# Last weight's low halves made by TensorE in the bank of its norms, in a one-core kernel of top-k attention and two ReLU² networks

## The chip, the cores and the metric

The program runs on one core of one Trainium2 chip. The metric is device time of one execution in microseconds. The kernel before takes 1182.04 us (median of three runs, 1180.84 to 1185.24).

## The reference, cut to what matters

```
q, k, v: (4, 8, 576, 64) f32       # batch, heads, sequence, head_dim
scores = q @ k.T / 8               # per batch and head
keep the 32 largest of each row of 576, softmax over them, attn = p @ v
x  = attn laid out as 2304 tokens x 512
x1 = (s * relu(x  @ moe_w_in )**2 + b) @ moe_w_out     # 512 -> 2048 -> 512
x2 =      relu(x1 @ moe2_w_in)**2      @ moe2_w_out    # 512 -> 2048 -> 512
```

The four weights arrive as 64-bit words (float64 bits). The kernel makes float32 of them on the chip.

## The kernel before, in words

The 2304 tokens are cut into 18 tiles of 128. Tile 4 and tile 13 (counted from 0) hold 64 rows each of two batches. For each tile the eight attention heads are done one by one, 144 in all; the text below counts heads from 1. A head is: Q times K on TensorE (`f_qk`, L594, into one of two `pS` banks), four rounds of the eight largest on VectorE (`max` L605, `match_replace` L616), exp on ScalarE (L619), the mask and the row sum on VectorE (L643), a float16 pair of high and low halves (ScalarE L646, GpSimd L451), a transposing DMA, and P times V on TensorE (`f_av`, L659).

A tile that has its eight heads goes to network 1 (`ffn(u, 0, ...)`) and later to network 2 (`ffn(u, 1, ...)`). The units of tiles are named F00 to F014 for network 1 (eleven single tiles, three pairs, one single) and F10 to F19 for network 2 (one single, eight pairs, one single). A unit has 16 chunks of the inner 2048: twelve matmuls in (`f_in`, L762), ReLU and two squares on ScalarE (L771, L773, L776), the low half on GpSimd (L781), and three matmuls out for each tile (`f_out`, L799).

Every matrix product is made with float16 pairs (high half, low half). So each of the four weights, numbered 0 to 3, is prepared once, in 16 chunks of 128 x 512: a load; two or three VectorE operations that put the float64 bits together (L884, L893, L900), with ScalarE and GpSimd helping where the table `CONV` says T (L889, then L451 by `po27`); a `gram` matmul (`f_mm`, L947) that sums squares into the bank `pC[1]`; after each group of chunks (one group for weights 0 and 1, two for 2, four for 3) a scale from the largest column norm (`weight_scale`: L955, L957, L959); and then `split_w`, which writes the halves. `SPLIT` says how, chunk by chunk:

- O: ScalarE scales the chunk (L912) and casts it (L913), GpSimd subtracts (L451).
- U: ScalarE makes the high half (L915), GpSimd scales the chunk (L929) and subtracts (L451).
- P: ScalarE makes the high half (L915); TensorE forms the difference in a PSUM bank from a scaled diagonal `dgs` and minus one times the high half (`f_sub`, L922 and L923); ScalarE copies it out (L926).

Weights 0 and 1 are split by P, weight 2 by O and U in turn, weight 3 by O. Weight 3 is not kept on the chip: its halves are stored to device memory (`wo2`) and read back in pairs of chunks through the two `wring` buffers for every unit of network 2. `column_sums` (L1059) adds up weight 1's halves on TensorE, also in `pC[1]`, for the constant b of network 1.

Nothing runs in the order in which it is written. `Plan.add` records each operation with an engine, a cost, a priority, what it reads and what it writes; the order of writing alone sets the dependencies (a bank or buffer that two operations share). `Plan.order` then builds one fixed queue for each engine with a list scheduler that goes by costs and priorities. The priority is a number of heads, plus what the table `TW` adds for the operation's name and its tag. Each engine works through its queue in order and waits where its next operation isn't ready.

Of the kernel before, what the change touches and what calls it, by code (L numbers as in the profile page):

```python
# [34 lines left out]
SPLIT = ('P', 'P', 'OU', 'O')  # L35
# [7 lines left out]
HW = 1  # L43
# [4 lines left out]
X2F = 14  # L48
WB = 3
CSP = 12  # L50
# [3 lines left out]
LN = 9  # L54
WO2S = 0
# [8 lines left out]
QP = 8  # L64
# [214 lines left out]
def kernel(  # L279
# [191 lines left out]
    def pair_sums(b, j, prio, raws):  # L471
        for a, (raw, rn) in enumerate(raws):
            add(act, "ac1", 0.86, prio, lambda raw=raw, a=a: nc.scalar.activation(
                out=junk, in_=raw.rearrange("p c d -> p (c d)"), func=ACTF.Square,
                accum_out=kst[:, b, j, a:a + 1]), r=[rn, rn + "m"], w=[f"kst{b}{j}{a}"])
# [20 lines left out]
    def prep_pair(b, j, prio):  # L496
# [7 lines left out]
        for a, (raw, rn) in enumerate(raws):  # L504
# [8 lines left out]
            add(act, "ac3", 0.64, prio, lambda raw=raw, dst=dst: nc.scalar.copy(dst[:, :, 0, :], raw),  # L513
# [11 lines left out]
    def prep_q(t, prio):  # L525
# [15 lines left out]
        add(act, "ac4", c_act(DM), prio, lambda: nc.scalar.activation(  # L541
# [8 lines left out]
        add(act, "ac6", c_act(DM), prio, lambda: nc.scalar.copy(nat[:, :, 0, :], raw3), r=names, w=[nh])  # L550
# [116 lines left out]
    def split_x(n, prio, xt_i, tt, sc, si):  # L667
# [3 lines left out]
        add(act, "ac14", c_act(DM), prio, lambda: nc.scalar.activation(  # L671
# [5 lines left out]
        add(act, "ac16", c_act(DM), prio, lambda: nc.scalar.copy(nat[:, 0:DM], x), r=[f"xs{n}"], w=[f"xnh{n}"])  # L677
# [229 lines left out]
    def split_w(o, on, hi, lo, hn, ln, wi, c, prio):  # L907
# [20 lines left out]
        if way == "U":  # L928
            add(pool, "po29", 0.81, prio, lambda: nc.gpsimd.tensor_scalar(o, o, sc, None, op0=ALU.mult), r=[scn] + hn, w=on)  # L929
        on_pool("po30", prio, lo, o, hi, DM, HW, on + hn, ln)  # L930

    def gram_place(wi):

        if wi > 1 and "P" in SPLIT[wi]:
            return pH[:, 258:386], pH[:, 384:512], "pG"
        return pC[1][:, 0:128], pC[1][:, 384:512], "pC1"
# [220 lines left out]
```

## Time and profile before

| what | value |
|---|---|
| median of three runs | 1182.04 us |
| the profiled execution, its own time | 1180.55 us |
| its span in the profile | 1178.8 us |
| TensorE matmul busy | 1023.8 us (87%) |
| VectorE busy | 968.4 us (82%) |
| ScalarE busy | 878.8 us (75%) |
| GpSimd busy | 705.1 us (60%) |
| chain that ended last, by engine | PE 48%, DVE 10%, DMA 8%, ACT 6% |

The profile gives busy time of each engine over the whole span or over stretches of it, the groups of instructions with count and mean, what ended the idle time before each, and the chain of work that ended last. Shares over the whole span hide that the program has stages: weights and the first tiles (to about 320 us), attention with both networks beside it (to 1017 us), and a rest of network work alone.

### The profile page before, as it was taken

Reading aid. Unit: us, or ns where it says so; the run is one execution under the profiler, and the core shown is the slowest. Engines: PE = TensorE matmul, PEld = TensorE weight load, DVE = VectorE, ACT = ScalarE, POOL = GpSimd, SP = SyncE. Lnnn points to the kernel's source line nnn. Section 1 sums busy time; section 2 is a strip of 40 time slices with the busy share of each in tenths; the row PEclk is TensorE's granted clock in tenths of the full one; section 3 lists DMA queues with packets and bytes.
Section 4 is the critical chain, followed back from the end, with each engine's and each line's share of the span. In section 5 each row is a group of like instructions: output and inputs, shape, how many; then the busy total and the mean of one; then the engine's idle time right before and its main releaser. Section 6 shows DMA issues by size and latency. Waiting matters only on the chain.

```text
span 1178.8 us, 27766 instructions
## 1 busy us (share of the span) xinstructions
PE 1023.8 (87%) x10000; PEld 691.4 (59%) x10000; DVE 968.4 (82%) x2126; ACT 878.8 (75%) x2242; POOL 705.1 (60%) x1121
## 2 busy tenths in 40 slices
PE   1376757678989999998999999999999999999996
PEld 1233335446657667666666676666666676666664
DVE  6999999999998999999999999997999999510000
ACT  3478757779889878878997899868877687565644
POOL 4577299888667645755776567646654464442322
PEclk9979978889999999999999999999999999999999
DMA  8778954566966773585488636676386256233134
GB/s 256 236 227 204 232 168 116 161 179 157 221 126 134 164 174 65 122 203 139 92 151 199 133 75 131 160 175 123 79 165 159 50 144 166 46 69 121 28 115 145
DMA packets 338218, 171.16 MB, mean 145 GB/s; under 512 B 292512, under 2 KB 317088, under 8 KB 338080
## 3 DMA queue, kind: packets, MB, share of 16 engines
q1 hardware_dynamic: 338080, 169.39, 60.1%
q8 instruction: 78, 1.28, 0.5%
q14 instruction: 60, 0.49, 0.1%
HBM read 89.65 MB, written 8.91 MB: 84 GB/s over the span
## 4 chain that ended last, share of the span: by engine, by line
PE 48%; DVE 10%; DMA 8%; ACT 6%; issue 2%; POOL 2%; SPq 1%; POOLq 0%; ACTq 0%; DVEq 0%
PE pC L799 20%; PE pH L762 18%; DVE m L605 5%; PE pA L659 4%; DMA pT<-pn 4%; PE pC L762 3%; PE pS L594 3%; DMA wring<-wo 2%; DVE wk L616 2%; DVE spare L616 2%; DVE et L643 1%; ACT rr L771 1%; DMA xT<-xn 1%; DMA out_dram<-xs 1%; DMA qT<-knat 1%
## 5 line engine op out<-in xcount | busy, mean ns | idle before, releaser
L762 PEld LDWEIGHTS <-w 128*128 128x128 f16 x4800 | 366.2, 99 | 103.1 <-issue 40.9
L762 PE MATMUL pH<-xT,w 128*128 128x256 f16 (+1 forms) x3648 | 371.2, 252 | 23.5 <-ACT rr L771 19.3
L451 POOL TENSOR_TENSOR pn<-et,pn 128x576 f16<-128x576 f32 x144 | 185.8, 1292 | 49.0 <-ACT pn L646 35.3
L781 POOL TENSOR_TENSOR gl<-gg,gh 128x128 f16<-128x128 f32 (+1 forms) x216 | 116.3, 539 | 143.7 <-ACT gh L773 83.1
L771 ACT ACTIVATE rr<-pH,rsc 128x256 f32<-128x256 f32 (+1 forms) x304 | 128.8, 424 | 95.7 <-PE pH L762 93.1
L605 DVE MAX8 m<-wk 128x8 f32<-128x576 f32 x252 | 189.0, 750 | 1.2
L799 PE MATMUL pC<-wring,gh 128*128 128x512 f16 x576 | 171.4, 379 | 6.1 <-DMA wring<-wo 6.1
L799 PE MATMUL pC<-wo,gh 128*128 128x512 f16 x576 | 173.4, 383 | 2.3 <-ACT xs L822 2.1
L781 POOL TENSOR_TENSOR gl<-sqr,gh 128x128 f16<-128x128 f32 (+1 forms) x184 | 100.0, 544 | 115.3 <-ACT gh L773 66.2
L773 ACT ACTIVATE gh<-rr 128x128 f16<-128x128 f32 (+1 forms) x400 | 139.4, 352 | 22.9 <-PE pC L799 17.1
L799 PEld LDWEIGHTS <-gh 128*128 128x128 f16 x1152 | 102.9, 99 | 77.2 <-issue 10.3
L605 DVE MAX8 m<-spare 128x8 f32<-128x576 f32 x180 | 135.0, 750 | 0.9
L619 ACT ACTIVATE et<-pS,ngm,cq 128x576 f32<-128x576 f32 x144 | 118.5, 824 | 14.4 <-POOL pn L451 4.8
L616 DVE MATCH_REPLACE8 wk<-m,wk 128x576 f32<-128x576 f32 x168 | 124.6, 742 | 0.0
L605 DVE MAX8 m<-pS 128x8 f32<-128x576 f32 x144 | 108.6, 756 | 15.9 <-PE pS L594 15.0
L646 ACT CAST pn<-et 128x576 f16<-128x576 f32 x144 | 95.7, 665 | 29.7 <-DVE et L643 26.9
L643 DVE SCALAR_TENSOR_TENSOR et<-pS,m,et 128x576 f32<-128x576 f32 x144 | 115.7, 807 | 2.2
L799 PE MATMUL pC<-wo,gl 128*128 128x512 f16 x288 | 110.0, 382 | 3.6 <-POOL gl L781 3.5
L659 PEld LDWEIGHTS <-pT 128*128 128x128 f16 (+1 forms) x2400 | 88.9, 104 | 37.2 <-DMA pT<-pn 22.2
L799 PE MATMUL pC<-wring,gl 128*128 128x512 f16 x288 | 109.2, 379 | 0.0
L659 PE MATMUL pA<-vp,pT 128*128 128x64 f16 (+1 forms) x2400 | 96.9, 198 | 12.9 <-DMA pT<-pn 12.7
L799 PEld LDWEIGHTS <-gl 128*128 128x128 f16 x576 | 56.5, 98 | 76.2 <-POOL gl L781 9.3
(203 smaller groups left out, 1726.5 us busy)
## 6 DMA issues: line engine op xcount, KB each, us to landing
wring<-wo SPq DMA_DIRECT2D x80, 512.0 KB, 3.8
wring<-in_moe_w_out_dram SPq DMA_DIRECT2D x18, 512.0 KB, 4.2
wring<-in_moe_w_in_dram SPq DMA_DIRECT2D x17, 512.0 KB, 4.6
xT<-in_moe_w_in_dram SPq DMA_DIRECT2D x15, 512.0 KB, 5.4
xT<-in_moe_w_out_dram SPq DMA_DIRECT2D x14, 512.0 KB, 4.7
qW<-qT SPq DMA_DIRECT2D x36, 128.0 KB, 2.7
kvraw<-in_k_dram SPq DMA_DIRECT2D x16, 256.0 KB, 3.7
kvraw<-in_v_dram SPq DMA_DIRECT2D x16, 256.0 KB, 3.2
```

The costliest lines, as they stand in the source:

```text
L451: add(pool, step, c_pool(cols * (c.stop - c.start) / n), prio, lambda c=c: nc.gpsimd.tensor_tensor(o[:, c], x[:, c], y[:, c], op=op), r=r, ...
L605: add(dve, "dv10", 0.67, prio, lambda src=src, rd=rd: nc.vector.max(m[:, 8 * rd:8 * rd + 8], src), r=[sn], w=[f"m{i2}_{rd}"])
L616: add(dve, "dv11", 0.735, prio, lambda src=src, rd=rd: nc.vector.match_replace(wk, m[:, 8 * rd:8 * rd + 8], src, NEG), r=[sn, f"m{i2}_{rd} ...
L619: add(act, "ac9", 0.72, prio, lambda: nc.scalar.activation(out=e, in_=s, func=ACTF.Exp, bias=ngm[i2][:, 0:1], scale=cq[q2][:, j:j + 1]), r ...
L643: add(dve, "dv15", 0.73, prio, lambda: nc.vector.scalar_tensor_tensor(e, s, m[:, TOPK - 1:TOPK], e, op0=ALU.is_ge, op1=ALU.mult, accum_out ...
L646: add(act, "ac13", 0.575, prio + 0.5, lambda: nc.scalar.copy(pt[:, 0, o:o + S], e), r=[f"et{i2}"], w=[f"pn{i2}", f"pnh{i2}"])
L659: nc.tensor.matmul(pA[r0:r0 + n, h, :], lhsT=pT[p3][:, a * 5 + c, r0:r0 + n], rhs=vv[:, vc, z, :], start=(c == 0 and a == 0 and z == 0), s ...
L762: nc.tensor.matmul(ps_, lhsT=win[:, f, a, kk, :], rhs=x[:, z * KD + kk, :], start=(kk == 0 and a == 0 and z == 0), stop=(kk == KD - 1 and ...
L771: add(act, "ac18", 0.06 + n / 1200.0, prio, lambda r=r, pin=pin, rs=rs: nc.scalar.activation(out=r, in_=pin[:, 0:n], func=ACTF.Relu, scale ...
L773: add(act, "ac19", 0.094 + n / 1200.0, prio, lambda r=r, hi=hi: nc.scalar.activation(out=hi, in_=r, func=ACTF.Square), r=rrn, w=ghn)
L781: add(pool, "po19", 0.12 + n * 0.0021, prio, lambda gt=gt, hi=hi, lo=lo: nc.gpsimd.tensor_tensor(lo, gt, hi, op=ALU.subtract), r=gn + ghn, ...
L799: nc.tensor.matmul(pC[tt], lhsT=src[g3][:, c], rhs=wt(a), start=(f == 0 and a == 0 and src is gh), stop=(f == KF - 1 and src is gl))
```

## The change

- `SPLIT` of weight 2 is O throughout in place of O and U in turn: the eight GpSimd scalings (L929) go, and ScalarE scales and casts those chunks.
- `SPLIT` of weight 3 is P in place of O. TensorE forms its low halves, for each of the four groups in `pC[1]`, the bank in which that group's and the next group's norms are summed; `gram_place` now names that bank always. One more diagonal is made for each group (L965 of before).
- `column_sums` is written ahead of weights 2 and 3. All three use `pC[1]`, so the sums now come before weight 2's norms.
- Weight 3 is written after the ninth head's position (`WO2S` 8) and no more right behind weight 2.
- `X2F` 16: the result of network 1 for tiles 14 and 15 is taken out of PSUM by ScalarE with GpSimd adding, as for the tiles before them, and no more by VectorE.
- Costs that the scheduler uses, some offsets of priorities, and every number of `TW` are new, so all queues are in a new order.

```diff
-SPLIT = ('P', 'P', 'OU', 'O')
+SPLIT = ('P', 'P', 'O', 'P')
-X2F = 14
+X2F = 16
-CSP = 12
+CSP = 14
-LN = 9
-WO2S = 0
+LN = 4
+WO2S = 8
-QP = 8
+QP = 4
...
-    "A0.0": -9.1, "A0.1": 33.9, "A0.2": 50.1, "A0.3": -51.4, "A1.0": 23.4, "A1.1": 3.4, "A1.2": -5.7, "A1.3": -56.8,
+    "A0.0": -18.3, "A0.1": 33.6, "A0.2": 38.8, "A0.3": -60.0, "A1.0": 7.7, "A1.1": 17.4, "A1.2": -12.3,
...
-            add(act, "ac1", 0.86, prio, lambda raw=raw, a=a: nc.scalar.activation(
+            add(act, "ac1", 0.67, prio, lambda raw=raw, a=a: nc.scalar.activation(
...
-            add(act, "ac18", 0.06 + n / 1200.0, prio, lambda r=r, pin=pin, rs=rs: nc.scalar.activation(
+            add(act, "ac18", 0.14 + n / 1200.0, prio, lambda r=r, pin=pin, rs=rs: nc.scalar.activation(
...
-            add(act, "ac28", c_act(DM), prio, lambda: nc.scalar.copy(lo, pd), r=pdn[:1], w=ln)
+            add(act, "ac28", 0.47, prio, lambda: nc.scalar.copy(lo, pd), r=pdn[:1], w=ln)
...
-            add(pool, "po29", 0.81, prio, lambda: nc.gpsimd.tensor_scalar(o, o, sc, None, op0=ALU.mult), r=[scn] + hn, w=on)
+            add(pool, "po29", 1.55, prio, lambda: nc.gpsimd.tensor_scalar(o, o, sc, None, op0=ALU.mult), r=[scn] + hn, w=on)
...
     def gram_place(wi):
 
-        if wi > 1 and "P" in SPLIT[wi]:
-            return pH[:, 258:386], pH[:, 384:512], "pG"
         return pC[1][:, 0:128], pC[1][:, 384:512], "pC1"
...
         if t == 0:
             first_weights()
+            column_sums()
             late_weights()
-            column_sums()
             if WO2S < H:
                 late_weights2()
```

Three places show what the new queues look like. The first is GpSimd's queue at the split of weight 2 (`w_68`; `pn` are the heads' halves, `xT`, `wstg`, `vp` and `spare` the float32 chunks of weight 3). Before:

```order
109 L441 TENSOR_SCALAR wsc_172<-wsx_168 128x1
110 L929 TENSOR_SCALAR w_68<-w_68,wsc_172 128x512
111 L1024 TENSOR_SCALAR wsv_176<-wsv_176,wlh 128x2
112 L451 TENSOR_TENSOR w_68<-w_68 128x512 x2
113 L813 TENSOR_TENSOR usc_150<-xsc_142,fc 128x1
114 L929 TENSOR_SCALAR w_68<-w_68,wsc_172 128x512
115 L451 TENSOR_TENSOR pn_103<-et_101,pn_103 128x576
```

The same place of the change:

```order
119 L451 TENSOR_TENSOR spare<-spare,xT_108 128x512
120 L441 TENSOR_SCALAR wsc_173<-wsx_169 128x1
121 L1022 TENSOR_SCALAR wsv_176<-wsv_176,wlh 128x2
122 L443 TENSOR_SCALAR wsv_177<-wsi_165 128x1
123 L451 TENSOR_TENSOR w_68<-w_68 128x512 x7
124 L451 TENSOR_TENSOR pn_102<-et_100,pn_102 128x576
```

The scalings are gone, and the subtractions of weight 2 stand in one run, behind the first scale of weight 3 (`wsc_173`).

The second place is SyncE's DMA queue where weight 3's last chunks are stored (`wo_70<-kT`) and read back for F10 (`wring<-wo_70`); each `pT` transpose belongs to a head. Before:

```order
151 L412 DMA wo_70<-kT_78 128x1024
152 L412 DMA wo_70<-kT_79 128x1024
153 L649 DMA_TRANSPOSE pT_106<-pn_103 128x10x128
154 L412 DMA wo_70<-kT_78 128x1024
155 L412 DMA wo_70<-kT_79 128x1024
156 L649 DMA_TRANSPOSE pT_104<-pn_102 128x10x128
157 L518 DMA_TRANSPOSE kT_78<-knat 128x9x128
158 L412 DMA kvraw_87<-in_v_dram 128x64
159 L412 DMA kvraw_87<-in_v_dram 128x2x256
160 L412 DMA wring_72<-wo_70 128x2048
```

The same place of the change:

```order
153 L412 DMA wo_70<-kT_79 128x1024
154 L649 DMA_TRANSPOSE pT_105<-pn_103 128x10x128
155 L412 DMA wo_70<-kT_78 128x1024
156 L518 DMA_TRANSPOSE kT_78<-knat 128x9x128
157 L412 DMA wo_70<-kT_79 128x1024
158 L412 DMA kvraw_87<-in_v_dram 128x64
159 L412 DMA kvraw_87<-in_v_dram 128x2x256
160 L649 DMA_TRANSPOSE pT_106<-pn_102 128x10x128
161 L412 DMA wring_72<-wo_70 128x2048
```

The last store stands behind the transpose of the 26th head in place of the 24th, and the read that follows it behind that of the 27th in place of the 25th.

The third place is ScalarE's queue ahead of the exponential of the 31st head (L619); `rsc_181` is network 1, `rsc_182` network 2. Before:

```order
470 L773 ACTIVATE gh_115<-rr_111 128x128
471 L771 ACTIVATE rr_111<-pH,rsc_181 128x128
472 L773 ACTIVATE gh_116<-rr_112 128x128
473 L771 ACTIVATE rr_112<-pC_190,rsc_181 128x128
474 L773 ACTIVATE gh_114<-rr_111 128x128
475 L612 ACTIVATE ngm_125<-m_0_121,ncq_134 128x1
476 L776 ACTIVATE gg<-rr_111 128x128
477 L619 ACTIVATE et_100<-pS_185,ngm_125,cq_132 128x576
```

The same place of the change:

```order
457 L771 ACTIVATE rr_111<-pH,rsc_182 128x128
458 L776 ACTIVATE gg<-rr_111 128x128
459 L646 CAST pn_102<-et_100 128x576
460 L771 ACTIVATE rr_112<-pC_190,rsc_182 128x128
461 L612 ACTIVATE ngm_125<-m_0_121,ncq_134 128x1
462 L773 ACTIVATE gh_115<-rr_112 128x128
463 L776 ACTIVATE sqr<-rr_112 128x128
464 L581 ACTIVATE ncq_133<-cq_131 128x1
465 L619 ACTIVATE et_100<-pS_185,ngm_125,cq_132 128x576
```

At the same head the queue of before is in F02 (network 1), and that of the change still in F10 (network 2, which comes ahead of F02 in both).

## Rows read from the trace of the kernel before

**Rows 1.** Windows: busy us (instructions) by engine, clock, DMA share, GB/s
```profile
145.00:290.00 145.00, 98.42 (x1020) 66.20 (x1021) 139.98 (x292) 110.18 (x269) 132.71 (x164) 0.85 0.59 158
322.00:670.00 348.00, 326.75 (x3611) 228.22 (x3609) 332.55 (x752) 288.06 (x798) 217.97 (x390) 0.99 0.68 143
670.00:1008.00 338.00, 330.91 (x3258) 227.59 (x3257) 320.96 (x718) 265.48 (x664) 201.07 (x336) 1.00 0.56 127
1008.00:1175.00 167.00, 158.14 (x1301) 107.08 (x1298) 13.51 (x34) 92.58 (x247) 52.75 (x103) 1.00 0.31 90
```

**Rows 2.** Timeline: QK of heads 33, 89, 144; VectorE's last mask
```profile
322.37 0.42 PE L594 MATMUL pS<-kT,qT 128*64 128x512 f16 x2
...
668.81 0.38 PE L594 MATMUL pS<-kT,qT 128*128 128x512 f16 x1
...
1005.67 0.38 PE L594 MATMUL pS<-kT,qT 128*128 128x512 f16 x1
...
1016.40 0.81 DVE L643 SCALAR_TENSOR_TENSOR et<-pS,m,et 128x576 f32<-128x576 f32 x1
```

**Rows 3.** Waits of VectorE over the span: us, times, longest
```profile
DVE m L605 <- PE pS L594: 15.0, 26, 1.2
```

**Rows 4.** Groups of POOL, 145 to 290 us: busy, mean ns, idle before
```profile
L929 POOL TENSOR_SCALAR w<-w,wsc 128x512 f32<-128x512 f32 x7 | 12.9, 1843 | 0.9 <-ACT w L915 0.9
...
L451 POOL TENSOR_TENSOR kT<-xT,kT 128x512 f16<-128x512 f32 x6 | 7.1, 1189 | 1.2 <-ACT kT L913 1.2
...
L451 POOL TENSOR_TENSOR kT<-vp,kT 128x512 f16<-128x512 f32 x5 | 5.8, 1156 | 0.0
...
L451 POOL TENSOR_TENSOR kT<-wstg,kT 128x512 f16<-128x512 f32 x3 | 3.5, 1161 | 0.0
...
L451 POOL TENSOR_TENSOR kT<-spare,kT 128x512 f16<-128x512 f32 x2 | 2.3, 1152 | 0.0
L929 POOL TENSOR_SCALAR kT<-kT,wsc 128x512 f32<-128x512 f32 x1 | 1.7, 1749 | 0.0
```

**Rows 5.** Windows of lines L884, L893, L900 alone: VectorE's busy us (count)
```profile
145.00:290.00 145.00, 18.66 (x19) 0.85 0.59 158
...
145.00:290.00 145.00, 3.73 (x4) 0.85 0.59 158
...
145.00:290.00 145.00, 17.14 (x20) 0.85 0.59 158
```

**Rows 6.** Sources L884, L900, L965: ns of one, least/median/most, first and last start
```profile
L884 DVE TENSOR_SCALAR wstg<-xT x3: 411/452/478, 167.0 to 255.2; 128x512 int32<-128x512 int32 x3
...
L900 DVE SCALAR_TENSOR_TENSOR kT<-xT,kT x1: 666/666/666, 160.6 to 160.6; 128x512 int32<-128x512 int32 x1
...
L965 DVE TENSOR_SCALAR gg<-sqr,wsc x2: 271/271/271, 60.1 to 114.8; 128x128 f32<-128x128 f32 x2
```

**Rows 7.** Timeline, 255.6 to 260.5 us, VectorE and then POOL
```profile
256.27 3.70 DVE L884 TENSOR_SCALAR vp<-wring 128x512 int32<-128x512 int32 x1
...
256.80 1.27 POOL L451 TENSOR_TENSOR pn<-et,pn 128x576 f16<-128x576 f32 x1
...
258.41 1.27 POOL L451 TENSOR_TENSOR wstg<-wstg,xT 128x512 int32<-128x512 int32 x1
260.11 1.28 POOL L451 TENSOR_TENSOR vp<-vp,wring 128x512 int32<-128x512 int32 x1 [0.42 <-issue]
```

**Rows 8.** Timeline of TensorE: differences of weight 1, column sums, two chunks of F02
```profile
130.80 1.04 PE L922 MATMUL pH<-wo,gg 128*128 128x512 f32 x2
131.68 0.38 PE L923 MATMUL pH<-wo,minus 128*128 128x512 f16 x1
131.90 0.39 PE L947 MATMUL pC<-w 128*128 128x128 bf16 x4
...
165.00 7.72 PE L1059 MATMUL pC<-wo,ones 128*128 128x512 f16 x32 [0.46 <-DVE wsm L959]
...
318.95 0.83 PE L762 MATMUL pH<-xT,w 128*128 128x128 f16 x12
319.62 0.83 PE L762 MATMUL pC<-xT,w 128*128 128x128 f16 x12
```

**Rows 9.** Chain that ended last, 410 to 420 us: start, us, what
```profile
409.96 0.65 PE pC L799 x3
...
411.92 1.29 PE pC L799 x6
413.22 0.48 PE pA L659 x15
```

More of the change, by code (lines that the diff above doesn't have):

```diff
@@ L512, in prep_pair @@
                     out=raw, in_=raw, func=ACTF.Copy, scale=ksc[:, b, j, a:a + 1]), r=[f"ks{b}{j}"], w=[rn, rn + "m"])
-            add(act, "ac3", 0.64, prio, lambda raw=raw, dst=dst: nc.scalar.copy(dst[:, :, 0, :], raw),
+            add(act, "ac3", 0.57, prio, lambda raw=raw, dst=dst: nc.scalar.copy(dst[:, :, 0, :], raw),
                 r=[rn, rn + "m"], w=[dn + "h"])
@@ L540, in prep_q @@
         names = [rn, rn + "m"] + ([rn + "b"] if len(tiles[t]) == 2 else [])
-        add(act, "ac4", c_act(DM), prio, lambda: nc.scalar.activation(
+        add(act, "ac4", 0.62, prio, lambda: nc.scalar.activation(
             out=junk[:, :DM], in_=raw, func=ACTF.Square, accum_out=qsc[i2][:, 1:2]),
@@ L549, in prep_q @@
             out=raw, in_=raw, func=ACTF.Copy, scale=qsc[i2][:, 0:1]), r=[f"qs{i2}"], w=names)
-        add(act, "ac6", c_act(DM), prio, lambda: nc.scalar.copy(nat[:, :, 0, :], raw3), r=names, w=[nh])
+        add(act, "ac6", 0.51, prio, lambda: nc.scalar.copy(nat[:, :, 0, :], raw3), r=names, w=[nh])
         on_pool("po8", prio, nat[:, :, 1, :], raw3, nat[:, :, 0, :], DM, HW if t < HT else 1, names + [nh], [nl])
@@ L670, in split_x @@
         nat = xn[n]
-        add(act, "ac14", c_act(DM), prio, lambda: nc.scalar.activation(
+        add(act, "ac14", 0.62, prio, lambda: nc.scalar.activation(
             out=junk[:, :DM], in_=x, func=ACTF.Square, accum_out=xss[si]), r=[f"xs{n}"], w=[f"xss{si}"])
@@ L676, in split_x @@
             out=x, in_=x, func=ACTF.Copy, scale=sc[:, 0:1]), r=[f"xsc{si}"], w=[f"xs{n}"])
-        add(act, "ac16", c_act(DM), prio, lambda: nc.scalar.copy(nat[:, 0:DM], x), r=[f"xs{n}"], w=[f"xnh{n}"])
+        add(act, "ac16", 0.51, prio, lambda: nc.scalar.copy(nat[:, 0:DM], x), r=[f"xs{n}"], w=[f"xnh{n}"])
         add(pool, "po14", c_pool(DM), prio, lambda: nc.gpsimd.tensor_tensor(
@@ L890, in to_f32 @@
                     out=lo, in_=lo.bitcast(U32), func=ACTF.Copy, scale=2.0 ** -29), w=rn[:1])
-                on_pool("po27", prio, oi, oi, lo, DM, HW, rn, on, op=ALU.add)
+                on_pool("po27", prio, oi, oi, lo, DM * 1.13, HW, rn, on, op=ALU.add)
             else:
@@ L912, in split_w @@
             add(act, "ac25", 0.61, prio, lambda: nc.scalar.activation(out=o, in_=o, func=ACTF.Copy, scale=sc), r=[scn], w=on)
-            add(act, "ac26", c_act(DM), prio, lambda: nc.scalar.copy(hi, o), r=on, w=hn)
+            add(act, "ac26", 0.51, prio, lambda: nc.scalar.copy(hi, o), r=on, w=hn)
         else:
@@ L948, in f_mm @@
                                  stop=(c % per == per - 1 and kk == KD - 1))
-        add(pe, "pe7", 0.3, prio, f_mm, r=on, w=[pgn])
+        add(pe, "pe7", 0.22, prio, f_mm, r=on, w=[pgn])
     def weight_scale(wi, j, const_k, prio, mask=EXP_MASK):
```

76 rows, old and new, of the table TW are left out of this document.

## Prediction

> **What bounds the kernel now.** I read the profile in this order. First the windows by stage [rows 1]. From 145 to 290 us VectorE (139.98 of 145 us) and GpSimd (132.71) are both full, while TensorE is busy for 98.42 and ScalarE for 110.18. This is where weights 2 and 3 are prepared. From 322 to 1008 us VectorE and TensorE are both close to full: TensorE 326.75 of 348 us, then 330.91 of 338. After that only TensorE is loaded (158.14 of 167). Next the timeline [rows 2], for three marks: the QK of head 33 goes out at 322.37 us, that of head 89 at 668.81, that of head 144 at 1005.67, and the last mask is done on VectorE at 1017.2. So 56 heads take 346.4 us and the 55 after them 336.9, 6.2 and 6.1 us each. Then VectorE's waits [rows 3]: in the whole span it waited 15.0 us for QK. VectorE therefore sets the pace of the heads, and TensorE is only just able to follow. The end is the time of head 144 plus a rest of TensorE work that is queued behind it. The end can move in three ways: VectorE reaches head 33 earlier or later, TensorE stops being able to follow, or the rest behind head 144 changes.
>
> **The change, part by part.** The sum is made against the profiled execution, 1180.55 us; the median of the runs is 1.5 us above it.
>
> *GpSimd loses work.* Eight scalings go, 12.9 + 1.7 us, and the sixteen subtractions of weight 3, 7.1 + 5.8 + 3.5 + 2.3 us [rows 4]. That is 33.3 us, all in the stretch of 132.71 busy us [rows 1], a quarter of it. GpSimd itself ends nothing here, so this counts only through those it holds up. The one on the path is VectorE. Its three conversion lines take 18.66, 3.73 and 17.14 us for 19, 4 and 20 instructions [rows 5]. Undisturbed ones take 0.411 (L884) and 0.666 (L900, and I use it for L893, which has the same shape) [rows 6], so 7.8 + 2.7 + 13.3 = 23.8 us. The other 15.7 us are lost beside GpSimd. The longest case shows how: an L884 that needs 0.411 lasted 3.70, and GpSimd's subtraction, a product's low half and a conversion ran through it one behind the other, and it ended as GpSimd had its first gap [rows 7]. A quarter less GpSimd work would return 3.9 of the 15.7 us if the loss goes with busy time. A loss that ends at a gap shrinks faster than that, so I take **−6 us**; the bounds are 0 (the conversions that meet GpSimd are the same ones) and −15.7 (all of it).
> The Trainium skill (SBUF — State Buffer, section "SBUF: two separate sides") says that VectorE and GpSimd share a port pair as an exclusive lock, held for the whole instruction, and the other fully blocks. The row agrees on the block, not on its length, which spanned several GpSimd instructions. By that rule alone, with each conversion blocked by one instruction, the return would be the 3.9 us and the sum 2 us higher.
>
> *TensorE gains sixteen differences.* One is 1.10 us from its start to that of the next work (130.80 to 131.90) [rows 8], so 17.6 us. They stand in TensorE's queue between heads 18 and 28, where it is idle for 47 of 145 us [rows 1], so no cost there by time. But the queue shows that network work is pushed back: at the QK of head 33, five out-chunks of F10, one out-chunk and seven in-chunks of F02 that stood ahead of it now stand behind it, and one head's PV has come ahead. With 0.65 for an out-chunk and 0.48 for PV [rows 9], and 0.67 for an in-chunk (318.95 to 319.62) [rows 8], that is 6 x 0.65 + 7 x 0.67 − 0.48 = 8.1 us more behind head 33. At head 89 the two queues are level. So TensorE has to do 8.1 us more between these two marks. It is idle there for 21.2 of 348 us, and from 670 to 1008 us it kept VectorE's pace with 7.1 idle of 338 [rows 1]. There is room for all of it. As the idle pieces don't lie where the work does, I let 6 of the 8.1 disappear in them: **+2 us**, with bounds 0 and +8.1.
>
> *ScalarE* casts eight chunks of weight 2 more and copies out sixteen differences where it cast before, some 6 us more; it has 35 idle us in the stretch [rows 1], which cover it. Without that cover the exponentials would come late by up to those 6 us, and VectorE's masks with them.
>
> *VectorE* makes four more diagonals at 0.271 [rows 6], **+1 us**. The two results of network 1 that it no longer takes lay near or behind its last heads; the network 2 units that read them come a whole unit later, so nothing.
>
> *Column sums ahead of weight 2's norms.* 7.72 us of TensorE [rows 8], the same as before, in a stretch where it idles. Weight 2's scales come about two heads later. Nobody needs weight 2 before F10, and F10 needs weight 3 as well: its last stores stand two heads later in SyncE's queue, and the read behind them too. This delay of F10 is in the 8.1 us. The columns' result is needed only at the end of F00. Nothing more.
>
> *Moved queues.* SyncE's stores of weight 3 pass K and V loads of the second batches, which now start earlier; no wait of VectorE hangs on them in either order. Behind the QK of head 144 the new queue holds one out-chunk of a pair less (1.29 us [rows 9]): **−1 us**.
>
> Sum: −6 + 2 + 1 − 1 = **−4 us**: 1176.5 for a profiled execution, **1178** for the median.
>
> **The rivals.** *Forecast: no change that can be told* (0.5%, or 6 us, is about what a measurement of this kernel can tell), 1176 to 1188.
>
> *Faster: GpSimd's queue was the real brake.* For it: two engines full from 145 to 290 us, and a block of 3.70 us that ended only at GpSimd's gap [rows 7]. If all 15.7 us return and TensorE takes the 8.1 us wholly into its idle time, the sum is −15.7 + 1 − 1 = −15.7, so 1166 for the median. Against it: three of the four GpSimd neighbours in rows 7 stay. It decides from about 8 us returned, at 1176 and below.
>
> *Slower: one bank for norms and differences.* Weight 3 has four groups, and the norms of the next group can't start in the bank before the four differences of the last one have been made and copied out, on engines whose queues hold heads and network chunks between. TensorE has shown such a wait: the column sums started 0.46 us late, behind VectorE's read of the same bank [rows 8]. If three such changes of group each hold QK back by 1.2 us, the longest of VectorE's waits for it [rows 3], and GpSimd's relief brings nothing, and the 8.1 us find no idle place, the sum is 3.6 + 8.1 + 1 − 1 = +11.7, so 1194. It decides if TensorE's idle time between heads 33 and 89 stays at 21 us, and head 33 is no earlier. Against it: 47 idle us of TensorE in the stretch.
> The Trainium skill (PSUM — Partial Sum Buffer, section "PSUM bank collisions raise a hardware error") speaks against this change: it wants a bank guarded as a whole between engines, not by address, so a norm and a difference in one bank take turns even where their columns differ. By it the turns are certain and only their price is open: with the price above and nothing else changed the time would be 1182 + 3.6, about 1186.
>
> **How the numbers follow.** The forecast has most for it, as its terms are small and of both signs: 0.41. Faster: 0.37, as its two steps are partly shown. Slower: 0.22, since it needs several things to fail at once or an order that fits the chip worse somewhere that no row shows. The range goes from 1163 (the faster rival with a little for waits that a new order may save) to 1192 (nearly all of the slower one). The likeliest case's own range is 1176 to 1188.
>
> **What would show it.** Right: L929 gone; L884, L893 and L900 together some 34 us in place of 39.5 in their stretch; QK of head 33 at 316 to 318 us; TensorE's idle time between heads 33 and 89 down from 21 to about 15 us; the last mask about 1014 us, and 158 us from it to TensorE's end as before. Wrong: head 33 later than 322 us with QK waiting for the bank, or head 33 earlier by 10 us and more, or a last mask that moves by another amount than head 33 did.

## The result and the profile after

The changed kernel takes **1165.26 us** (median of 4 runs, 1163.23 to 1168.51) against 1181.44 before (1179.91 to 1185.24) on the same chip: ratio 0.9867, 95% interval 0.9851 to 0.9883. That is 1.3% faster, inside the range, at the time of the faster rival (1166) and not of the forecast (1178). The profiled execution has a span of 1163.9 us against 1178.8.

Where did the 14.9 us come from? Windows of the profile that end with the mask of head 32, of head 88 and of the last head (columns as in [rows 1]: length, then the busy us and instructions of TensorE, its weight loads, VectorE, ScalarE and GpSimd, then TensorE's granted clock, the DMA share and GB/s). Before:

```profile
0.00:325.70 325.70, 211.09 (x1868) 130.34 (x1868) 304.89 (x633) 234.87 (x544) 235.24 (x297) 0.90 0.75 196
325.70:671.80 346.10, 325.41 (x3594) 227.58 (x3595) 330.75 (x749) 287.15 (x795) 216.84 (x388) 0.99 0.67 142
671.80:1017.20 345.40, 338.31 (x3327) 232.74 (x3325) 328.40 (x733) 269.15 (x671) 202.76 (x337) 1.00 0.55 125
```

After, with the tail:

```profile
0.00:311.80 311.80, 209.81 (x1805) 124.03 (x1807) 296.34 (x634) 229.62 (x526) 195.68 (x265) 0.92 0.76 197
311.80:652.60 340.80, 331.75 (x3712) 233.38 (x3713) 328.97 (x752) 293.15 (x822) 220.97 (x397) 1.00 0.70 151
652.60:1003.60 351.00, 341.92 (x3329) 233.56 (x3327) 327.29 (x735) 268.22 (x672) 205.65 (x339) 1.00 0.58 123
1003.60:1163.90 160.30, 147.76 (x1210) 100.34 (x1208) 3.63 (x12) 86.19 (x235) 51.00 (x100) 1.00 0.30 92
```

The four lengths change by −13.9, −5.3, +5.6 and −1.3 us (the tail was 1178.8 − 1017.2 = 161.6). VectorE's busy time is the third pair; what is left of a stretch is its waits. Up to head 32 it is busy for 8.6 us less and waits for 15.5 us in place of 20.8. From there to head 88 TensorE has 6.3 us more to do in 5.3 us less, so its idle time falls from 20.7 to 9.1 us. From head 88 on VectorE waits 6.7 us more.

The 8.6 us are the conversions. Windows of lines L884, L893 and L900 alone (VectorE's busy us and instructions), up to the mask of head 32, before:

```profile
0.00:325.70 325.70, 42.70 (x64) 0.90 0.75 196
0.00:325.70 325.70, 19.76 (x24) 0.90 0.75 196
0.00:325.70 325.70, 56.52 (x64) 0.90 0.75 196
```

The same lines after, and then in the stretch of [rows 5]:

```profile
0.00:311.80 311.80, 36.88 (x64) 0.92 0.76 197
0.00:311.80 311.80, 19.36 (x24) 0.92 0.76 197
0.00:311.80 311.80, 54.22 (x64) 0.92 0.76 197
...
145.00:290.00 145.00, 11.66 (x21) 0.93 0.68 171
145.00:290.00 145.00, 3.65 (x5) 0.93 0.68 171
145.00:290.00 145.00, 17.96 (x22) 0.93 0.68 171
```

The same 152 instructions take 118.98 us before and 110.46 after: −8.5. In the stretch 33.27 us are left, of which 48 undisturbed ones [rows 6] would need 8.6 + 3.3 + 14.7 = 26.6. So 6.7 us are lost beside GpSimd, where it was 15.7 [rows 5]. VectorE's waits over the whole span, next to [rows 3]:

```profile
DVE m L605 <- PE pS L594: 16.3, 26, 2.1
DVE qsa L437 <- ACT junk L541: 7.6, 3, 3.5
DVE xs L717 <- PE pA L659: 4.8, 3, 3.9
```

QK is waited for as often as before and 1.3 us longer. The waits of 3 to 4 us in the other two rows lie behind head 33. Up to head 32 VectorE waits for GpSimd itself for 8.9 us before and 5.4 after. These rows of before are gone:

```profile
DVE xT L884 <- POOL kT L451: 1.4, 1, 1.4
DVE wo L900 <- POOL wo L451: 1.2, 1, 1.2
DVE vp L900 <- POOL vp L451: 0.5, 1, 0.5
DVE xT L900 <- POOL xT L451: 0.5, 1, 0.5
```

In the first a conversion waits until a subtraction of weight 3 has read the buffer that it writes; in the others it waits for GpSimd's part of the same conversion.

### The profile page after: what moved, and what is told of

Read it like the earlier page. It is cut to its first block, busy times and chain, and to the rows that moved or that the text cites. A ratio compares the mean times of both kernels' runs of the same rounds, so it can differ in the third digit from the quotient of the medians.

```text
span 1163.9 us, 27826 instructions
## 1 busy us (share of the span) xinstructions
PE 1031.2 (89%) x10048; PEld 691.3 (59%) x10048; DVE 956.2 (82%) x2128; ACT 877.2 (75%) x2252; POOL 673.3 (58%) x1099
## 5 line engine op out<-in xcount | busy, mean ns | idle before, releaser
L451 POOL TENSOR_TENSOR pn<-et,pn 128x576 f16<-128x576 f32 x144 | 186.7, 1299 | 51.5 <-ACT pn L646 38.9
L773 ACT ACTIVATE gh<-rr 128x128 f16<-128x128 f32 (+1 forms) x400 | 140.2, 353 | 15.8 <-PE pC L799 10.8
L619 ACT ACTIVATE et<-pS,ngm,cq 128x576 f32<-128x576 f32 x144 | 118.9, 827 | 10.0 <-POOL pn L451 2.3
L659 PEld LDWEIGHTS <-pT 128*128 128x128 f16 (+1 forms) x2400 | 85.0, 101 | 35.1 <-DMA pT<-pn 19.5
L659 PE MATMUL pA<-vp,pT 128*128 128x64 f16 (+1 forms) x2400 | 93.4, 194 | 11.0 <-DMA pT<-pn 10.5
L594 PE MATMUL pS<-kT,qT 128*128 128x512 f16 (+2 forms) x320 | 84.3, 297 | 20.8 <-DVE et L643 19.0
```

The source lines that it names most:

```text
L451: add(pool, step, c_pool(cols * (c.stop - c.start) / n), prio, lambda c=c: nc.gpsimd.tensor_tensor(o[:, c], x[:, c], y[:, c], op=op), r=r, ...
L594: nc.tensor.matmul(s[r0:r0 + n, c0:c0 + cn_], lhsT=w[:, h, r0:r0 + n], rhs=kk[:, k0:k0 + cn_], start=(a == 0), stop=(a == 1))
L619: add(act, "ac9", 0.72, prio, lambda: nc.scalar.activation(out=e, in_=s, func=ACTF.Exp, bias=ngm[i2][:, 0:1], scale=cq[q2][:, j:j + 1]), r ...
L659: nc.tensor.matmul(pA[r0:r0 + n, h, :], lhsT=pT[p3][:, a * 5 + c, r0:r0 + n], rhs=vv[:, vc, z, :], start=(c == 0 and a == 0 and z == 0), s ...
L773: add(act, "ac19", 0.094 + n / 1200.0, prio, lambda r=r, hi=hi: nc.scalar.activation(out=hi, in_=r, func=ACTF.Square), r=rrn, w=ghn)
```

## The experiments

Two theories. **Load:** what GpSimd no longer does near the late weights is what saves. **Order:** the new table saves, whatever GpSimd does. To part them, most runs hold the order: the scheduler plans with the kernel's own operations and costs, and only what is emitted at an operation's place is another. The kernel before ran beside each kernel below, so that these are set against the change by their ratios to it. All in one table, read as above (time; end of head 32's mask; VectorE busy up to there; its waits, which is the rest of that stretch; the three conversion lines):

| run | us | ratio to before, 95% | head 32 | busy | waits | conversions |
|---|---|---|---|---|---|---|
| before | 1181.4 | | 325.7 | 304.9 | 20.8 | 119.0 |
| after | 1165.3 | 0.9867 (0.9851–0.9883) | 311.8 | 296.3 | 15.5 | 110.5 |
| e1 | 1175.6 | 0.9962 (0.9948–0.9976) | 316.4 | 299.8 | 16.6 | 114.7 |
| e2 | 1183.8 | 1.0031 (1.0014–1.0047) | 332.3 | 297.9 | 34.4 | 111.0 |
| e3 | 1192.5 | 1.0095 (1.0068–1.0122) | 322.4 | 303.6 | 18.8 | 114.7 |
| e4 | 1192.5 | 1.0113 (1.0076–1.0150) | 314.9 | 299.1 | 15.8 | 112.0 |
| e5 | 1177.5 | 0.9960 (0.9944–0.9975) | 327.0 | 297.8 | 29.2 | 111.3 |
| e6 | 1176.7 | 0.9958 (0.9941–0.9975) | 325.7 | 297.5 | 28.2 | 111.0 |
| e7 | 1172.5 | 0.9930 (0.9914–0.9947) | 317.3 | 296.2 | 21.1 | 109.8 |
| e8 | 1175.6 | 0.9957 (0.9939–0.9974) | 311.0 | 296.1 | 14.9 | 110.4 |
| e9 | 1173.9 | 0.9945 (0.9926–0.9964) | 322.9 | 300.3 | 22.6 | 113.9 |
| e10 | 1165.9 | 0.9872 (0.9844–0.9900) | 314.3 | 296.8 | 17.5 | 111.1 |
| e11 | 1162.9 | 0.9844 (0.9816–0.9873) | 310.9 | 295.4 | 15.5 | 109.8 |
| e12 | 1163.5 | 0.9850 (0.9813–0.9888) | 315.2 | 297.7 | 17.5 | 111.9 |

**e1, the kernel before with less on GpSimd, order held.**

```diff
-            add(pool, "po29", 0.81, prio, lambda: nc.gpsimd.tensor_scalar(o, o, sc, None, op0=ALU.mult), ...)
+            add(pool, "po29", 0.81, prio, lambda: None, ...)
-        on_pool("po30", prio, lo, o, hi, DM, HW, on + hn, ln)
+            w = DM if c < 2 else 1      # weight 3 only
+            ... nc.gpsimd.tensor_tensor(lo[:, 0:w], o[:, 0:w], hi[:, 0:w], op=ALU.subtract)
```

> The kernel before with its order of instructions held on every engine; only GpSimd does less. The eight scalings of the third weight's odd chunks (12.9 + 1.7 us before) are dropped, and of the fourth weight's sixteen subtractions the last fourteen write one column of 512 (some 16 us less). What it leaves out: those low halves do not hold the remainder of their weight, so the corrections that they carry are missing from the product. Theory 1 (GpSimd's load beside VectorE is what cost the time): VectorE's lost time in the fourth weight's conversions falls from 14.5 us to under 9, the long blocks (3.70, 3.52 us) go, and the time falls by 7 to 11 us, to 1170 to 1174. Theory 2 (the new order is what saves): no more than 2 us either way, 1179 to 1183.

GpSimd was busy for 27.9 us less up to head 32, and that head was 9.3 us earlier: 4.2 us of conversions, 4.2 us of waits. So the load alone, here 27.9 of the 39.6 us that the change takes off GpSimd up to head 32, gives two thirds of the 13.9 us. But only 0.4% is left at the end, since in the old order 3.0 us are given back between heads 33 and 88 (349.1 us for them). The time lies between the two lines: neither theory is enough alone.

**e2, the change with load put back, order held.**

```diff
             nc.scalar.copy(lo, pd)
+            nc.gpsimd.tensor_scalar(lo, lo, 1.0, None, op0=ALU.mult)    # weight 3
...
+        for _ in range(1 + c % 2):                                      # weight 2
             nc.gpsimd.tensor_tensor(lo, o, hi, op=ALU.subtract)
```

> The changed kernel with its order held; only GpSimd is given back load that changes no value: the odd chunks of the third weight are subtracted twice, and each low half of the fourth weight is multiplied by one in place after ScalarE has written it (eight subtractions and sixteen multiplications, about 8 x 1.1 + 16 x 0.8 = 22 us). Theory 1 (GpSimd's load): VectorE's lost time comes back, by two thirds of the load that was removed: 5 to 9 us slower than the changed kernel, 1170 to 1174. Theory 2 (order): 1163 to 1168, the same as the changed kernel.

Some 19 us slower than the change, twice the most that theory 1 allowed, and in another way: the conversions take 0.6 us more, and that is all. The time is lost in VectorE's waits, 15.5 to 34.4 us. Three of the four largest rows of them up to head 32 are:

```profile
DVE et L643 <- ACT et L619: 5.3, 2, 3.8
DVE vp L900 <- POOL vp L451: 4.2, 2, 2.7
DVE xT L900 <- POOL xT L451: 2.7, 2, 1.9
```

All rows of waits for GpSimd itself come to 14.3 us (5.4 after the change), those for exponentials to 8.9 (1.0). This gave the third theory, **queue**: GpSimd is itself the brake, and what waits for it is late.

**e3 and e4, the new way of making low halves with the old table, and the old way with the new table.** Here the scheduler plans anew.

```diff
-SPLIT = ('P', 'P', 'OU', 'O')     # e3, in the kernel before, with gram_place in pC[1]
+SPLIT = ('P', 'P', 'O', 'P')
...
-SPLIT = ('P', 'P', 'O', 'P')      # e4, in the changed kernel
+SPLIT = ('P', 'P', 'OU', 'O')
```

> The kernel before with one part of the change: the fourth weight's low halves by TensorE in the bank of the norms, the third weight's scaling by ScalarE, all with the table of offsets of before, so that the planner places the new work by the old offsets. Theory 1 (load): most of the gain, 7 to 11 us, 1170 to 1174. Theory 2 (order, by the new table): 1178 to 1186, since the table is the old one. The rival of the prediction that one bank for norms and differences costs a chain of waits: 1190 or more.

> The changed kernel with the old way of making low halves (third weight's odd chunks scaled by GpSimd, fourth weight's differences by GpSimd), and everything else of the change: the new table, the column sums ahead. Theory 1 (load): most of the gain is lost, 1174 to 1182. Theory 2 (order): 1164 to 1169.

Both are 1% slower than the kernel before, so neither theory holds by itself. Both have head 32 earlier than before, by 3.3 and 10.8 us, and lose it later. e3's time is at the line that its expectation set for the rival of one bank (1190 or more), but its trace shows no such chain: head 32 is not late, and between heads 33 and 88 QK is waited for 5.7 us where it was 5.9. e3 loses in single waits; VectorE's timeline (idle time ahead in brackets):

```profile
370.62 0.16 DVE L437 TENSOR_SCALAR xsa<-xss 128x1 int32<-128x1 int32 x1 [10.15 <-ACT junk L671]
...
819.12 0.15 DVE L437 TENSOR_SCALAR qsa<-qsc 128x1 int32<-128x1 int32 x1 [9.07 <-ACT junk L541]
```

e4 has one such wait too:

```profile
815.40 0.15 DVE L437 TENSOR_SCALAR qsa<-qsc 128x1 int32<-128x1 int32 x1 [9.41 <-ACT junk L541]
```

but most of its loss, 15.5 us, lies between heads 33 and 88, where TensorE has 18.9 us more to do than before (busy for 344.3 of 361.6 us). Waits of VectorE there:

```profile
DVE m L605 <- PE pS L594: 18.0, 16, 5.3
```

A small step of a scale stands in VectorE's queue ahead of masks and waits for ScalarE. The longest such wait after the change is 3.5 us. So a table of one set of operations left such places, and work in the wrong stretch, when it was used with another.

**e5, e6 and e9, one half of the old way at a time, order of the change held.**

```diff
-                nc.tensor.matmul(pd, ...)                               # e5, e9: weight 3
+                nc.gpsimd.tensor_tensor(lo, o, hi, op=ALU.subtract)     # e9 here, e5 where ScalarE copied
...
+            if c % 2: nc.gpsimd.tensor_scalar(o, o, sc, None, op0=ALU.mult)    # e6: weight 2
             nc.gpsimd.tensor_tensor(lo, o, hi, op=ALU.subtract)
```

> The changed kernel with its order held; the fourth weight's low halves alone go back to GpSimd: its 16 subtractions (about 1.17 us each, 18.7 us) stand where ScalarE's copies of the low halves stood, and TensorE's 17.6 us of differences are gone. Theory A (what the change saved is VectorE's lost time beside GpSimd): VectorE's lost time in the fourth weight's conversions rises from 6.5 us to over 10, 4 to 8 us slower than the changed kernel, 1169 to 1173. Theory B (GpSimd's own in-order queue had no room left there, and what waits behind it came late): VectorE's lost time hardly changes, its waits grow, 10 to 18 us slower, 1175 to 1183. Theory C (TensorE's 17.6 us were what the change paid): as fast as the changed kernel or faster, 1158 to 1166.

> The changed kernel with its order held; the third weight's odd chunks alone go back to the old way, scaled in place by GpSimd (8 times, 12.9 us in the profile before) ahead of their subtraction, ScalarE relieved of 8 x 0.5 us. Theory A (lost time): 2 to 4 us slower than the changed kernel, 1167 to 1170. Theory B (GpSimd's queue): nearly the whole 13 us, if these scalings stand in the stretch in which GpSimd has no room (150 to 230 us), 8 to 13 us slower, 1173 to 1178.

> The run with the fourth weight's low halves by GpSimd, mended. There each subtraction stood at the place of ScalarE's copy, behind the refill of the buffer that it reads, so that it took a later chunk's words and also waited for them; here it stands at the place of TensorE's difference, ahead of the refill. GpSimd has 16 x 1.17 = 18.7 us more, TensorE 17.6 us less, the order is held. Theory A (lost time of VectorE): 1169 to 1173, with over 10 us lost in the fourth weight's conversions. Theory B (GpSimd's queue): 1174 to 1180, lost time under 8 us, waits of VectorE in heads 9 to 24 up by 8 us or more. If the late place of the subtraction made the first run slow, it comes to under 1168.

In e5 some subtractions read their buffer after its refill, so those low halves belong to a later chunk; e9 is the run to go by. In both ScalarE scales weight 3's chunks in place and casts them, as in the kernel before, in place of writing the high half at once and copying the differences out. e6 costs 11 us for 13 us of scalings, hardly any of it in the conversions: queue. e9 costs 9 us for 18.7 us of subtractions; up to head 32 the conversions take 3.5 us more and the waits 7.2: queue first, lost time second (waits for GpSimd itself 9.0 us in place of 5.4, for exponentials 3.7 in place of 1.0). The times of e5 and e9 differ by no more than their intervals.

A second way by which a us on GpSimd becomes a wait of VectorE, through ScalarE, is seen in e6. Its GpSimd, with hardly a gap (L945 scales, L946 subtracts):

```profile
191.43 1.59 POOL L945 TENSOR_SCALAR w<-w,wsc 128x512 f32<-128x512 f32 x1
193.10 2.27 POOL L946 TENSOR_TENSOR w<-w 128x512 f16<-128x512 f32 x2
195.35 1.57 POOL L945 TENSOR_SCALAR w<-w,wsc 128x512 f32<-128x512 f32 x1
197.00 2.27 POOL L946 TENSOR_TENSOR w<-w 128x512 f16<-128x512 f32 x2
```

its ScalarE's waits, 185 to 215 us (L920 writes a high half, L922 casts):

```profile
ACT w L920 <- POOL w L946: 7.3, 5, 1.6
ACT w L922 <- POOL w L946: 1.9, 4, 1.0
```

and its VectorE's, 150 to 290 us:

```profile
DVE et L643 <- ACT et L619: 7.2, 2, 5.2
```

ScalarE may write a high half only when GpSimd has read the float32 chunk whose place it takes. Its queue stands there for 9.2 us, the exponentials behind it come late, and the masks wait for them. How full GpSimd is shows in windows of 40 us from 150 us on (GpSimd is the fifth pair). Before:

```profile
150.00:190.00 40.00, 24.61 (x210) 15.91 (x209) 39.37 (x78) 24.29 (x51) 39.82 (x38) 0.71 0.55 158
190.00:230.00 40.00, 28.38 (x307) 18.21 (x305) 37.37 (x78) 29.58 (x75) 38.22 (x49) 0.93 0.56 142
```

after:

```profile
150.00:190.00 40.00, 23.07 (x231) 15.51 (x230) 39.30 (x89) 26.08 (x52) 26.61 (x30) 0.82 0.64 181
190.00:230.00 40.00, 32.45 (x324) 20.95 (x324) 38.58 (x85) 36.14 (x93) 33.96 (x49) 0.92 0.64 154
230.00:270.00 40.00, 31.69 (x328) 19.63 (x327) 39.48 (x86) 31.91 (x79) 25.98 (x37) 1.00 0.79 196
270.00:310.00 40.00, 38.57 (x488) 28.11 (x486) 38.95 (x96) 36.87 (x109) 25.32 (x49) 1.00 0.70 154
```

Before, GpSimd had 2 us free of 80; after, 19.4. VectorE does 174 instructions there in place of 153. The same waits of ScalarE for GpSimd, from 145 to 290 us, are in the kernel before:

```profile
ACT w L912 <- POOL wsc L441: 4.0, 1, 4.0
ACT et L619 <- POOL pn L451: 3.5, 5, 1.6
ACT w L915 <- POOL w L451: 3.0, 5, 1.2
ACT w L913 <- POOL w L451: 2.0, 3, 0.8
```

and after:

```profile
ACT gg L776 <- POOL gl L781: 1.7, 3, 0.7
ACT et L619 <- POOL pn L451: 1.2, 3, 0.5
ACT w L913 <- POOL w L451: 0.2, 1, 0.2
```

All such rows together come to 17.9 us before and 5.9 after. Little of the 17.9 reached VectorE by way of the exponentials: up to head 32 it waited for them for 0.4 us before and for 1.0 after. What the change itself took away there are the waits for GpSimd shown in the section on the result; the way through ScalarE is shown by e2 and e6 alone.

**e7 and e10, the differences made twice, and not at all.**

```diff
+                for _ in range(2 if wi == 3 else 1):        # e7
                 nc.tensor.matmul(pd, lhsT=dgs[d], rhs=o, start=True, stop=False)
...
+                if wi == 3: return                          # e10, ahead of the two matmuls
```

> The changed kernel with its order held; TensorE makes each difference of the fourth weight twice into the same place (16 x 1.1 = 17.6 us more of TensorE ahead of head 33), nothing else. If TensorE has room ahead of head 33, as the prediction said of 9.5 of its 17.6 us, the time rises by 0 to 3 us, 1163 to 1168. If each us on TensorE there is a us of backlog, by 8 to 17 us, 1173 to 1182. A second load also keeps the granted clock up, which may give back 1 to 2 us.

> The changed kernel with its order held, without TensorE's products of the fourth weight's differences (16 x 1.1 = 17.6 us); ScalarE copies what stands in the bank, so that weight's low halves are not its remainders. With the run of doubled differences it gives the price of TensorE's work there. If the 17.6 us cost what the prediction took (+2 us): 1162 to 1165. If TensorE's work is paid as in the doubled run (0.3 us of each): 1158 to 1161. If the chain that the difference adds between ScalarE's two copies is what counts: 1155 or less.

Without the 17.6 us of differences the kernel is not faster (0.9872 against 0.9867); with them doubled it is 7 us slower. e10 lies just above its first line, e7 between its two. e10's second and third window:

```profile
190.00:230.00 40.00, 30.61 (x310) 21.93 (x310) 36.74 (x81) 34.54 (x90) 31.55 (x47) 0.78 0.64 152
230.00:270.00 40.00, 23.56 (x286) 17.76 (x284) 38.66 (x80) 30.84 (x76) 27.02 (x36) 0.87 0.71 188
```

Where TensorE has less to do, its granted clock is lower: 0.78 and 0.87 in place of 0.92 and 1.00, that is, parts of the stretch at 1.2 GHz in place of 2.4. e5 and e9, also without the differences, have 0.83 and 0.79, 0.80 and 0.84; e7, e8 and e11, with them, 0.92 or 0.93, and 1.00. Up to head 32 TensorE is busy for 198.4 us, only 11.5 less than the change for 17.6 us less work, and VectorE waits 2 us longer. Whether the clock or TensorE's idle time made the removal worth nothing is not parted by these runs. In e7 the cover is gone in the last window, where TensorE is full and VectorE no longer is:

```profile
270.00:310.00 40.00, 38.84 (x431) 26.71 (x430) 34.20 (x87) 32.84 (x98) 22.30 (x46) 1.00 0.57 130
```

VectorE waits for QK for 6.5 us up to head 32 there, 1.2 after the change. So the first 17.6 us were free and the next cost 0.4 us each.

**e12, the column sums twice; e11, GpSimd relieved further.**

```diff
+            for _ in range(2):                                           # e12
                 for f in range(KF): ...
...
-        on_pool("po30", prio, lo, o, hi, DM, HW, on + hn, ln)            # e11, weight 2
+        add(pool, "po30", c_pool(DM), prio, lambda: nc.gpsimd.memset(lo, 0.0), r=on + hn, w=ln)
```

> The changed kernel with its order held; the column sums, which the change put ahead of the late weights, are made twice (7.7 us more of TensorE at that place). If the place is hidden: 0 to 1 us, 1164 to 1167. If the sums hold up the bank that the next weight's norms need, so that its scales and everything behind come late: 4 to 8 us slower, 1169 to 1173.

> The changed kernel with its order held, GpSimd relieved further: the third weight's 16 subtractions (1.17 us each, 18.7 us) become 16 settings of the low halves to zero, so that this weight's corrections are left out. If GpSimd's queue still sets the pace of heads 9 to 24: 3 to 8 us faster than the changed kernel, 1157 to 1162. If the change has brought GpSimd below its limit and VectorE's own work sets the pace: 0 to 3 us faster, 1162 to 1166.

Both intervals overlap that of the change. The place of the sums is hidden, even for twice their work; here too the clock rose with the work (150 to 190 us, 0.92 where the change had 0.82). Behind it, from 230 to 270 us, it was lower than in the change, 0.91 in place of 1.00, and that cost nothing that can be told either:

```profile
150.00:190.00 40.00, 28.26 (x264) 17.31 (x263) 39.90 (x90) 25.59 (x51) 26.73 (x31) 0.92 0.66 176
...
230.00:270.00 40.00, 32.14 (x309) 20.32 (x309) 37.71 (x79) 30.41 (x73) 26.15 (x36) 0.91 0.81 187
```

In e11 GpSimd is busy for 185.4 us up to head 32 in place of 195.7, and head 32 comes 0.9 us earlier. A third of e1's relief gives a tenth of its 9.3 us: the change has taken GpSimd below its limit, and VectorE's own work is left (39.8, 37.3, 39.6 and 38.9 of 40 us in e11's windows).

**e8, the late waits behind head 33.**

```diff
+EARLY = {'K13': 4.0, 'K33': 4.0, 4493: 3.0}     # us; 4493 is the last product of head 96
-        for i in self.order():
+        key = {i: self.st[i] - EARLY.get(i, EARLY.get(self.tags[i], 0.0)) for i in self.order()}
+        ...                                      # emitted by key, dependences first
```

> The changed kernel with its order held but for three places behind head 33, where VectorE waited 3.4 to 5.5 us in one piece: the preparation of the key pairs for heads 39 and 111 (K13, K33) is emitted 4 us earlier, and the last product of head 96 3 us earlier on TensorE. If those waits are on the path: 3 to 8 us faster than the changed kernel, 1157 to 1162. If TensorE's work bounds there (334 of 343 us busy): no change, 1163 to 1167.

Ten us slower, the opposite of both lines. The moved steps' data was not there yet. ScalarE in e8:

```profile
339.79 0.68 ACT L488 ACTIVATE junk<-kvraw 128x576 bf16<-128x576 f32 x1 [2.82 <-DMA kvraw<-in_v_dram]
...
788.03 0.68 ACT L488 ACTIVATE junk<-kvraw 128x576 bf16<-128x576 f32 x1 [2.94 <-DMA kvraw<-in_v_dram]
```

and the first of them after the change, at the same time and without a wait:

```profile
340.03 0.67 ACT L473 ACTIVATE junk<-kvraw 128x576 bf16<-128x576 f32 x1
```

The step ran no earlier, and all that stood behind it in ScalarE's queue came 3 us late; head 32 is 0.8 us earlier than in the change, the last mask 14.0 us later. The two stalls make 5.8 us of this; where the rest arose was not followed. No version here is faster than the change beyond the intervals; e11 leaves out part of the work, and e12 only adds some.

## Why the prediction was right, and where it was wrong

- *What bounds.* Right that VectorE sets the pace and that the stretch up to head 33 decides. Wrong in "GpSimd itself ends nothing here, so this counts only through those it holds up. The one on the path is VectorE": the two full engines of [rows 1] were read as one bound and its neighbour. In windows of 40 us GpSimd has 0.2 and 1.8 us free, and VectorE itself waited for it for 8.9 us up to head 32, 5.4 after. e2 and e6 put load back: VectorE's waits rise by 18.9 and 12.7 us, directly and through ScalarE's exponentials, and the conversions by no more than 0.6. This step failed: the term had no place for waits, and their fall gave 5.3 us up to head 32, 3.5 of them waits for GpSimd.
- *The −6 us of lost time.* Right in kind, too small: −8.5 us measured. In the stretch of [rows 1] GpSimd's busy time fell by 23% (132.71 to 102.54 us) and the lost time by 57% (15.7 to 6.7), more than proportional as argued; no conversion of the trace after is longer than 1.77 us, where [rows 7] had 3.70. The 3.9 us that were set beside the Trainium skill's rule (SBUF — State Buffer, "SBUF: two separate sides") are less than half of what came. That all of the 8.5 us is due to the load is not shown: with the order held, less load returns 4.2 us (e1), and load put back into the new order takes 0.6 (e2), 0.5 (e6) and 3.5 (e9).
- *The +2 us of TensorE.* It was −5.3 from head 32 to head 88. The work pushed back went wholly into idle time, as the faster rival had it, and VectorE's waits fell by 3.5 us besides. That the differences themselves cost nothing was right (e10); besides the idle time that the prediction gave as the reason, the clock fell without them, which it did not have.
- *ScalarE, the column sums, the diagonals.* ScalarE's 6 us are covered: its waits for GpSimd fell by 12.0 us. The sums' place is free (e12). The +1 of the diagonals can't be told apart.
- *The tail, −1 us.* −1.3 measured.
- *Heads 89 to 144.* The prediction gave no term to the new order there; it cost 5.6 us, in VectorE's waits for TensorE: for QK 11.3 us in place of 7.5, for PV (L717) 4.5 in place of 0.5, 3.9 of them in one piece. Which part of the order made TensorE late was not tried.
- *The sum.* −4 forecast; −13.9 − 5.3 + 5.6 − 1.3 = −14.9 came. The range holds the result because the faster rival was in it; the forecast's own range, 1176 to 1188, does not, and the prediction's own sign of being wrong, head 33 earlier by 10 us and more, came (13.9 us by the mask of head 32). The faster rival's time was right; its mechanism half: 8.5 of 15.7 us returned, and up to head 32 waits made up most of the rest. That the total met its −15.7 so closely is in part luck: the +5.6 and −5.3 us behind head 32, for which it had no term, cancel. The slower rival fell: without the differences in the bank the time is the same (e10). The Trainium skill's rule (PSUM — Partial Sum Buffer, "PSUM bank collisions raise a hardware error") agrees with the trace on the turns, as TensorE waits five times, 4.5 us in all, for ScalarE's copies out of the bank (L922 behind L926); the 1186 worked out beside it did not come.

Still open: how much of the 16 us a table fitted anew to the old way would also find. This is the rival that no run excludes. With the order held the load is worth 9.3 us at head 32 and 5 at the end in the old order (e1), 9 and 11 us by halves in the new (e9, e6). e3 and e4 show that each way is slower with the other's table; they don't show what a refitted old way would reach. That the sums' place gains anything was not tried alone.

## What to carry to other kernels

Look at two full engines in short windows: if the second has no gap either, price its work as a queue, with all that waits for it directly or through a third engine, and not only as a disturbance of the first. Where an order is fitted to its operations, change one thing with the order held before you judge it; a mixed version measures the misfit. A step emitted earlier than its data stalls everything behind it on its engine.

## What the hardware showed unexpectedly

TensorE's granted clock went with its work. Taking 17.6 us of matmuls away lowered it in the 80 us from 190 us on from 0.92 and 1.00 to 0.78 and 0.87 (e10; e5 and e9 alike) and saved nothing; adding 7.7 us raised it from 0.82 to 0.92 in its window (e12, 150 to 190 us; all other traces of this order had 0.82 to 0.87) and cost nothing, though it was lower than in the change from 230 to 270 us. These are windows of one trace each: over the whole span the clock of four runs was 0.965 to 0.977 for the change, 0.966 to 0.972 for e10 and 0.978 to 0.985 for e12. Load added to GpSimd hardly lengthened VectorE's conversions in e2 (110.5 to 111.0 us) although it added 19 us of waits; in e9 it lengthened them by 3.5 us.
